# Moving a gate's logit into a projection's spare column, in a fused state-space and linear-attention kernel with a hand-ordered instruction list

## The chip, the cores and the metric

The kernel runs on one core of a Trainium2 chip. The metric is the device time of one execution in microseconds (us); the kernel is launched once per execution. The core has five instruction queues that run side by side and meet at semaphores: PE (matrix multiply), DVE (vector), ACT (scalar and table functions), POOL and SP (here a queue that issues DMA transfers).

## The reference

Two layers read the same kind of input and a gate mixes them, with `x` of 2048 positions by 512:

```python
g = sigmoid((x * gate_w).sum(-1, keepdims=True))
a = S5(x)              # h[t] = Lam_bar * h[t-1] + B_bar x[t];  y = 2 Re(C h) + x * Dskip
b = hedgehog(x)        # linear attention, 32 heads of 16
out = g * a + (1 - g) * b

# hedgehog: pq = q @ w_phi, pk = k @ w_phi (per head)
phi_q = cat(softmax(pq), softmax(-pq));  phi_k = cat(softmax(pk), softmax(-pk))
kv = phi_k^T v;  z = sum(phi_k);  o = (phi_q kv) / (phi_q z + 1e-6);  b = o @ wo
```

The two inputs `A_x` and the B layer's weights are bf16; the S5 layer has 512 complex states.

## The kernel before

**Tiles.** The 2048 positions lie in 16 tiles of 128; `order` gives the tile that step n of the output works on. `x` is kept transposed in `xT`. The weights of K and Q are folded with `w_phi` first (`st_W` transposes K's weight, `fold` multiplies, `st_f` for K and `st_w` for Q), so that one multiplication gives the features' logits, 15 relative columns for each of 32 heads, 480 in all.

**Steps.** Each step is a Python generator that issues a few instructions at each `next`: `k`, `v`, `q` project a tile (`tile_mm`, L483) and evict it from PSUM (`evac`: L129 on ACT, L131 on DVE); `x`, `n`, `e`, `s` (and `X`, `N`, `E`, `S` for Q) make the softmax features of a group of tiles on DVE and ACT (the exponential is L554); `S` ends with a transpose by DMA. `a` adds a tile to the K-V matrix in two PSUM banks that are held through it all (`live["acc"]`). `b`, `g`, `z`, `H`, `h`, `p`, `c` are the state-space layer: input products (L613, L625), the recurrence as a scan, and scalings (`scaled`: L436 on ACT, L438 on DVE). In the last third `y` multiplies states and C for a tile (L816), adding the skip term by a diagonal matrix `Dd` (L823), `o` makes numerator and denominator of the attention (L835, with a logarithm L839 and an exponential L842 for the division, and the multiplication L848), `O` transposes its result by DMA (L862), `t` multiplies by `wo` into the same bank as `y` and evicts it scaled by the gate (L875; L881 on ACT, L883 on DVE), and `R` stores it.

**The gate.** The logit of a tile is four matmuls of one column, with `gw_b` as the moving operand, into a spare column of the second K-V bank, issued with each tile of `a` (L603). After the last tile one step `G` makes the clamped, negated logit `nge` and the factor `G` (1 + exp) for all 16 tiles. `o` uses `nge` as a bias of its exponential (L842), `t` scales by `G`.

**The skip term.** For the tiles in `XD`, steps 8 to 14, it doesn't go through PE: `Ld` loads x untransposed into the space of K's and V's weights, `u` multiplies x by G and Dskip on DVE (L854), and `t` adds it (L879, on DVE).

**The order.** Nothing is scheduled by the machine: the string `ORDER` is a list of step names, and each name issues that step's next part. On each engine the instructions run in that order. `@` gives a step's PSUM banks (8 banks; `o` takes two neighbours), `:D` puts its eviction or scaling on DVE instead of ACT. A planner outside the kernel searched the list. `Z` is a matmul on zeros, of no use to the result. `Lk`, `Lx`, `Lv`, `Lq`, `Lb`, `Lc`, `Ld`, `Lo` issue loads from SP: K's weight, x, V's weight, Q's weight, B, C, the rows for `u`, and `wo`. `V` transposes the state-space parameters on PE (L321), `P` to `P4`, `M`, `U` and `i` work on them and make cosine and sine tables (`T2c`, `T2s`).

Of the kernel before, what the change touches and what calls it, by code (L numbers as in the profile page):

```python
# [10 lines left out]
ALU = mybir.AluOpType  # L11
AX = mybir.AxisListType
ACT = mybir.ActivationFunctionType
F32 = mybir.dt.float32
# [10 lines left out]
Lk Lk Z@0 B:D B Z Z Z Z Z B B W01@1 Lx Z W00@2 Lx W00 W00 W01 W01:D Lx W11@3 W10@4 W11 Z B f1@5 f1 Lv f0@1 T1@0 W10:D  # L25
f0:D T0@3 f2@2 T1 Lx T0:D f3@4 f3:D Lx f2 k1@6 Lx V@7 k0@3 V P k1 k1 U P U P2 Lx P2 U P2 P2 U P2 P4 P3 P4 k0 k0 n0 P4
x0 P P2 P3 i1 k2@7 k3@6 k2 k3 x0 i1 i1 x0 n0 i0 i1 i0 V2@3 V2 i1 M x0 k5@4 i0 k7@5 k7 i0 n0 k4@2 k4 x0 v1@6 k5 n0 i0
v1 i3 M k6@7 i3 x1 k6 i2 v5@2 i3 i3 i3 v5 i2 M v0@4 Lx Lx x1 Lb k8@5 n0 v0 i2 i2 i2 n1 L e0 x1 n1 x1 M gw v3@7 k15@4
n1 D v6@6 k15 Lb k9@2 v3 k8 b000@3 k11@0 k11 Lb b100@4 n1 x1 n1 b010@5 D x2 Lb s0 e1 n2 s0 n2 b100 Lq Lq b011@7 k10@0
b001@1 s0 x2 s0 s0 Lc b000 b101@3 x2 w3@4 k9 s0 n2 k13@2 x2 k10 b011 Lo n2 x2 n2 g001@7 M2 b010 b001 Lc e2 s1 x3 s1 n3  # L30
k14@5 x3 g000@1 v6 w1@0 s1 g001 x3 g000 n3 k13 s1 n3 g010@2 c1:D c1:D Lc Lc e2 g001 g010 s0 g000 s1 g011@6 g011 x0z:D
x3 n3 k14 c2 b101 D s1 s2 c2:D s2 g011 g010 g010 D g011 s2 a0@51 a0 c0 v2@7 w3 g011 g011 k12@3 c0:D w0@4 v2 g010 k12
g010 w2@6 w2 s2 g100@7 g100 x3 s2 n3 c3 c3:D x4 w1 Ld z0 z0 b110@6 x4 z0 n4 z0 w0 z0 n4 b111@2 g101@4 g101 s1 b110 z0
e3 g101 n4 q2@6 z0 n4 z0 q1@0 c3:D x4 z0 x4 e3 s3 z0 s3 g100 b111 c0 a1 a1 g111@4 s2 x4 n4 q3@3 g111 g111 g111 g110@2
H0:D g110 g110 q2 H0 c2 Ld Ld g110 s3 q0@6 b211@7 H0 s3 q1 s2 H0 g110 c0 q0 b201@0 q3 g110 c1 X0 N0 g111 g111 v7@6 H0
z1 z1 X0 s3 b200@2 g201@4 b201 N0 c2 v7 z1 X0 z1 z1 z1 s3 N0 b211 z1 b200 z1 g200@0 b210@6 g201 q4@7 e4 b210 X0 v4@2
# [12 lines left out]
S3 S3 y8 o10 p31 t8 o11@6 O3 t9 S3 S3 t6 o11 o11 p21 p31 t8 t9 y12@1 t7 p31:D y14@0 t6 t7 o11 o12@6 o12 p21 O5 p21
o13@2 u11 p31 y14 o12 o12 o13 y12 o13 R2 o14@6 o13 O6 o14 o14 o14 R4 u10 O7 y13@2 y13 o15@6 o15 o15 o15 t10 t10 R3 t11  # L50
t13 t11 u12 O8 u13 t12 t12 t13 u14 R5 t14 t14 R6 y15@54 y15 y15 t15 t15:D t15 R7 t15 R8 R8
# [4 lines left out]
XD = (8, 9, 10, 11, 12, 13, 14)  # L56
# [14 lines left out]
def kernel(  # L71
# [88 lines left out]
    Wq2 = const.tile([P, KT, DF], BF16, name="Wq2")  # L160
# [3 lines left out]
    gw_b = const.tile([P, KT], BF16, name="gw_b")  # L164
# [275 lines left out]
    def fold(W2, WT, dtile):  # L440
        pf = bank([P, DF], F32, "pf")
        for j in range(KT):
            MM(out=pf[:, j * DF // KT:(j + 1) * DF // KT], lhsT=WT[:, j, dtile * P:(dtile + 1) * P], rhs=BD[:, j].rearrange("p g f -> p (g f)"), start=True, stop=True)
        yield
        evac(W2[:, dtile, :].rearrange("p (hh f hl) -> p hh f hl", hh=8, f=Dh - 1), pf[:].rearrange("p (hh hl f) -> p hh f hl", hh=8, hl=4))
        yield
# [144 lines left out]
    def st_a(n):  # L591
        first, L = KGROUPS[n]
        for u in range(L):
            n_ = first + u
            ti = KO[n_]
            if n_ == 0:
                live["acc"] = [bank([P, 512], F32, f"kvacc{b}") for b in range(2)]
            for m in range(NB):
                MM(out=acc(m), lhsT=live["EE", n][:, u, m].rearrange("p s f -> p (s f)"),
                   rhs=vxb[n_ % NVX][:, 4 * m:4 * m + 4, :].rearrange("p h e -> p (h e)"),  # L600
                   start=(n_ == 0 and m % 4 == 0), stop=(n_ == NTI - 1), skip_group_check=True)
            for kt in range(KT):
                MM(out=live["acc"][1][:, 4 * KVW + ti:4 * KVW + ti + 1], lhsT=xT[:, kt, ti * P:(ti + 1) * P],  # L603
                   rhs=gw_b[:, kt:kt + 1], start=False, stop=(n_ == NTI - 1 and kt == KT - 1), skip_group_check=True)
            yield
# [137 lines left out]
    def st_G():  # L743
        VS(out=nge[:], in0=live["acc"][1][:, 4 * KVW:4 * KVW + NTI], scalar1=-Z_MAX, scalar2=-1.0, op0=ALU.max, op1=ALU.mult)
        yield
        aexp(out=G[:], in_=nge[:], func=ACT.Exp)
        yield
        VS(out=G[:], in0=G[:], scalar1=1.0, scalar2=None, op0=ALU.add)
        yield
        nc.vector.reciprocal(out=G[:], in_=G[:])  # L750
        yield
# [75 lines left out]
    def st_o(n):  # L827
        ti = order[n]
        op_ = pools["op"][1]
# [7 lines left out]
        yield  # L837
        ld = op_.tile([P, 2, 16], F32, name="ld")
# [3 lines left out]
        aexp(out=rd[:], in_=ld[:], func=ACT.Exp, scale=-1.0, bias=nge[:, ti:ti + 1])  # L842
# [8 lines left out]
    def st_u(n):  # L851
        ti = order[n]
        live["xd", n] = pools["op"][1].tile([P, D], F32, name="xd", bufs=2)
        nc.vector.scalar_tensor_tensor(out=live["xd", n][:], in0=xl(n), scalar=G[:, ti:ti + 1], in1=Drow[:], op0=ALU.mult, op1=ALU.mult)  # L854
        yield
# [10 lines left out]
    def st_t(n):  # L866
        ti = order[n]
# [5 lines left out]
        for py, (c, w) in zip(pys, [(0, D)] if len(pys) == 1 else LASTCUT):  # L873
            for g in range(HG):
                MM(out=py[:], lhsT=oT[:, g, :], rhs=Wo[:, g, c:c + w], start=False, stop=(g == HG - 1))  # L875
            yield
            ot = live["ot", g_][:, u, c:c + w]
            if n in XD:
                nc.vector.scalar_tensor_tensor(out=ot, in0=py[:], scalar=G[:, ti:ti + 1], in1=live["xd", n][:, c:c + w], op0=ALU.mult, op1=ALU.add)  # L879
            elif sel["eng"] == "act":  # L880
                nc.scalar.mul(out=ot, in_=py[:], mul=G[:, ti:ti + 1])  # L881
            else:
                VS(out=ot, in0=py[:], scalar1=G[:, ti:ti + 1], scalar2=None, op0=ALU.mult)  # L883
            yield

    def st_R(g):
# [3 lines left out]
        for (c, w), q in zip(LASTCUT if last else [(0, D)], (nc.sync, nc.scalar)):  # L890
# [4 lines left out]
          "M": st_M(), "M2": st_M2(), "D": st_D(), "L": st_L(), "G": st_G(), "Y": st_Y(), "END": st_END(), "Z": st_Z(), "x0z": st_x0(),  # L895
# [59 lines left out]
```

## Time and profile before

| | |
|---|---|
| median of 3 runs | 150.96 us (150.81 to 151.14) |
| the profiled execution | span 149.4 us from the first to the last instruction; no other time of this execution is given |
| PE, busy share | 142.8 us, 96%, 1010 matmuls |
| DVE | 139.0 us, 93%, 338 instructions |
| ACT | 125.1 us, 84%, 222 instructions |
| POOL | 26.6 us, 18%, 42 instructions |
| TensorE clock granted | 1.000 of full speed throughout |
| traffic | 20.14 MB in 52959 packets |

A row of the timeline gives the start, the duration of a run of like instructions, engine, line, operation, and what was written from what. An instruction's own record overlaps with the next one's on the same engine, so the time that it keeps its engine is better read from start to start. In a row of windows stand, after the bounds, the length and the busy time (with the number of instructions) of PE, its weight loads, DVE, ACT and POOL, then the granted clock, the DMA share and GB/s. In the chain of work that ended last a row is start, duration and what the chain ran through.

### The profile page before, as it was taken

How to read it: one execution, taken by the hardware profiler on the slowest of the kernel's cores; microseconds unless marked ns; L12 is line 12 of the kernel's file. 1: busy time of each engine (PE TensorE's matmuls, PEld its weight loads, DVE VectorE, ACT ScalarE, POOL GpSimd, SP SyncE). 2: the span in 40 equal slices, each digit the busy share in tenths (PEclk: the TensorE clock that was granted, in tenths of full speed). 3: DMA queues.
4: the chain of work that ended last, by engine and by line, in shares of the span. 5: the costliest groups of instructions: out<-in, count | busy, mean ns of one | idle time of the engine just before them, and what ended most of it. 6: DMA issues, size and time to landing. Idle time of an engine off the chain costs nothing.

```text
span 149.4 us, 2839 instructions
## 1 busy us (share of the span) xinstructions
PE 142.8 (96%) x1010; PEld 73.8 (49%) x1010; DVE 139.0 (93%) x338; ACT 125.1 (84%) x222; POOL 26.6 (18%) x42
## 2 busy tenths in 40 slices
PE   6999999999999999999999999999999999999980
PEld 2844444545545444464444467555444554455450
DVE  2899999999999999999999999999999999986880
ACT  3479999999999999999999999999989996552000
POOL 7403700000000341022605236011004200000000
PEclk9999999999999999999999999999999999999999
DMA  4999999991220174008274999908999996998742
GB/s 118 222 235 174 142 202 176 246 189 33 54 91 0 26 114 77 0 0 140 38 107 70 166 175 183 210 7 133 103 238 218 184 186 77 227 207 197 209 148 71
DMA packets 52959, 20.14 MB, mean 135 GB/s; under 512 B 44496, under 2 KB 52432, under 8 KB 52944
## 3 DMA queue, kind: packets, MB, share of 16 engines
q1 hardware_dynamic: 48000, 15.44, 53.1%
q0 software_dynamic: 4000, 4.20, 18.6%
q10 hardware_dynamic: 944, 0.31, 0.8%
q8 instruction: 8, 0.13, 0.4%
q14 instruction: 7, 0.06, 0.1%
HBM read 2.91 MB, written 2.10 MB: 33 GB/s over the span
## 4 chain that ended last, share of the span: by engine, by line
ACT 67%; PE 24%; issue 3%; DVE 2%
ACT EE L554 15%; PE PS L816 11%; ACT Xq L129 9%; PE PS L875 7%; ACT CT L436 6%; ACT vx L129 5%; ACT dg L436 4%; ACT H L129 3%; ACT vv L129 3%; ACT eb L129 3%; ACT Bn L129 3%; PE PS L316 2%; PE PS L835 2%; ACT lg L562 2%; ACT m L436 1%
## 5 line engine op out<-in xcount | busy, mean ns | idle before, releaser
L554 ACT ACTIVATE EE<-EE 128x2048 bf16<-128x2048 bf16 x16 | 32.5, 2066 | 0.2 <-DVE EE L548 0.2
L483 PE MATMUL PS<-WKV,xT 128*128 128x480 bf16 (+1 forms) x128 | 29.3, 373 | 0.2 <-DMA xT<-in_A_x_dram 0.2
L483 PEld LDWEIGHTS <-xT 128*128 128x128 bf16 x192 | 18.1, 98 | 19.4 <-DMA xT<-in_A_x_dram 0.7
L129 ACT CAST Xq<-PS 128x480 bf16<-128x480 f32 x32 | 20.1, 735 | 0.5 <-PE PS L483 0.5
L625 PE MATMUL PS<-xT,BT 128*128 128x512 bf16 x64 | 15.9, 379 | 0.0
L816 PE MATMUL PS<-C,H 128*128 128x512 bf16 x64 | 15.4, 378 | 0.5 <-DVE on L848 0.2
L875 PE MATMUL PS<-Wo,oT 128*128 128x512 bf16 (+2 forms) x68 | 15.5, 367 | 0.0
L613 PE MATMUL PS<-xT,BT 128*128 128x512 bf16 x64 | 15.4, 379 | 0.0
L483 PE MATMUL PS<-Wq,xT 128*128 128x480 bf16 x64 | 15.1, 366 | 0.0
L848 DVE TENSOR_TENSOR on<-PS,rd 128x512 bf16<-128x512 f32 x16 | 10.7, 681 | 2.3 <-ACT rd L842 2.3
L881 ACT ACTIVATE ot<-PS,G 128x512 bf16<-128x512 f32 (+1 forms) x8 | 4.9, 639 | 9.1 <-PE PS L875 9.1
L436 ACT ACTIVATE CT<-H,dgs 128x1024 bf16<-128x1024 bf16 x9 | 12.1, 1349 | 0.0
L129 ACT CAST vx<-PS 128x512 bf16<-128x512 f32 x16 | 11.7, 793 | 0.0
L648 POOL DMA_DIRECT2D C<-CT x4 | 5.4, 1352 | 35.0 <-ACT rc L566 31.8
L531 DVE TENSOR_TENSOR sm<-EE 128x2048 bf16<-128x2048 bf16 (+1 forms) x9 | 10.0, 1108 | 0.1
L542 DVE TENSOR_TENSOR EE<-Xq,mx 128x2048 bf16<-128x2048 bf16 (+1 forms) x9 | 10.0, 1109 | 0.0
L548 DVE TENSOR_TENSOR EE<-mn,Xq 128x2048 bf16<-128x2048 bf16 (+1 forms) x9 | 10.0, 1107 | 0.0
L613 PEld LDWEIGHTS <-BT 128*128 128x128 bf16 x64 | 6.3, 98 | 7.2 <-issue 0.2
L569 DVE TENSOR_TENSOR EE<-EE,rc 128x2048 bf16<-128x2048 bf16 x8 | 9.8, 1234 | 0.0
L625 PEld LDWEIGHTS <-BT 128*128 128x128 bf16 x64 | 6.1, 98 | 7.0
L875 PEld LDWEIGHTS <-oT 128*128 128x128 bf16 x68 | 6.1, 98 | 6.5 <-DMA oT<-on 0.5
L531 DVE TENSOR_TENSOR sm<-sm 128x512 bf16<-128x512 bf16 (+2 forms) x18 | 9.3, 516 | 0.0
(185 smaller groups left out, 325.8 us busy)
## 6 DMA issues: line engine op xcount, KB each, us to landing
out_dram<-ot SPq DMA_DIRECT2D x7, 256.0 KB, 2.4
C<-CT POOLq DMA_DIRECT2D x4, 256.0 KB, 3.9
eb<-CT POOLq DMA_DIRECT2D x4, 256.0 KB, 4.9
eb<-dg POOLq DMA_DIRECT2D x4, 256.0 KB, 5.9
WKV<-in_A_x_dram SPq DMA_DIRECT2D x3, 256.0 KB, 3.1
WKV<-in_B_wqkv_dram SPq DMA_DIRECT2D x1, 512.0 KB, 5.6
Wo<-in_B_wo_dram SPq DMA_DIRECT2D x1, 512.0 KB, 4.8
H<-CT POOLq DMA_DIRECT2D x2, 256.0 KB, 3.3
```

The lines of the kernel that those rows point to most:

```text
L129: nc.scalar.copy(out=out_ap, in_=in_ap)
L436: nc.scalar.mul(out=out_ap, in_=in_ap, mul=s_)
L483: MM(out=pt[:], lhsT=xT[:, kt, ti * P:(ti + 1) * P], rhs=W[:, kt, :], start=(kt == 0), stop=(kt == KT - 1))
L531: VT(out=dst, in0=cur[:, :, :, 0:n, :], in1=cur[:, :, :, n:2 * n, :], op=op)
L542: VT(out=half(EE, 0), in0=X5, in1=live["mx", p].to_broadcast([P, L, 8, Dh, 4]), op=ALU.subtract)
L548: VT(out=half(live["EE", p], 1), in0=live["mn", p].to_broadcast([P, L, 8, Dh, 4]), in1=X5, op=ALU.subtract)
L554: aexp(out=EE[:, l_:l_ + 2], in_=EE[:, l_:l_ + 2], func=ACT.Exp)
L613: MM(out=pb[:], lhsT=BT[:, ri, kt, j * P:(j + 1) * P], rhs=cells(kt, 2 * pr), start=(kt == 0), stop=(kt == KT - 1))
L625: MM(out=pgq[:], lhsT=BT[:, ri, kt, js], rhs=cells(kt, r1), start=(kt == 0), stop=False)
L816: MM(out=py[:], lhsT=hs[j][ri], rhs=C2[:, 1 - ri, j, c:c + w], start=(j == 0 and ri == 0), stop=False)
L848: VT(out=live["on", g_][:, u], in0=pn[:, :, :, 0:Dh], in1=rd[:].unsqueeze(3).to_broadcast([P, 2, 16, Dh]), op=ALU.mult)
L875: MM(out=py[:], lhsT=oT[:, g, :], rhs=Wo[:, g, c:c + w], start=False, stop=(g == HG - 1))
```

## The change

The gate's weight becomes a 481st column of Q's folded weight, so that the logit of a tile comes out of `q`, in the same bank, and is evicted by itself into `nge` (one column; an extra part of step `q`). `a` loses its four small matmuls. `G` becomes four steps, each for four tiles. `nge` and `G` are indexed by the step's number instead of the tile's. `XD` becomes the steps 8 to 11: steps 12, 13 and 14 get their skip term by `Dd` on PE again, lose `u`, and their `t` is a plain scaling. `ORDER` is a new list throughout, with other places, banks and engines for most steps.

```diff
-XD = (8, 9, 10, 11, 12, 13, 14)
+XD = (8, 9, 10, 11)
-    Wq2 = const.tile([P, KT, DF], BF16, name="Wq2")
+    Wq2 = const.tile([P, KT, DF + 4], BF16, name="Wq2")
     def st_gw():
-        nc.vector.tensor_copy(out=gw_b[:], in_=vec[:, 4, :])
+        nc.vector.tensor_copy(out=Wq2[:, :, DF], in_=vec[:, 4, :])
...
     def st_q(n):
-        pq = bank([P, DF], F32, "pq")
+        pq = bank([P, DF + 1], F32, "pq")
         tile_mm(pq, order[n], Wq2)
         yield
-        evac(xrel(n), pq[:].rearrange("p (hh x) -> p hh x", hh=8))
+        evac(xrel(n), pq[:, 0:DF].rearrange("p (hh x) -> p hh x", hh=8))
+        yield
+        evac(nge[:, n:n + 1], pq[:, DF:DF + 1])
         yield
...
     def st_a(n):
-            for kt in range(KT):
-                MM(out=live["acc"][1][:, 4 * KVW + ti:4 * KVW + ti + 1], lhsT=xT[:, kt, ti * P:(ti + 1) * P],
-                   rhs=gw_b[:, kt:kt + 1], start=False, stop=(n_ == NTI - 1 and kt == KT - 1), skip_group_check=True)
...
-    def st_G():
-        VS(out=nge[:], in0=live["acc"][1][:, 4 * KVW:4 * KVW + NTI], scalar1=-Z_MAX, scalar2=-1.0, op0=ALU.max, op1=ALU.mult)
-        yield
-        aexp(out=G[:], in_=nge[:], func=ACT.Exp)
+    def st_G(g):
+        ns = slice(4 * g, 4 * g + 4)
+        VS(out=nge[:, ns], in0=nge[:, ns], scalar1=-Z_MAX, scalar2=-1.0, op0=ALU.max, op1=ALU.mult)
+        yield
+        aexp(out=G[:, ns], in_=nge[:, ns], func=ACT.Exp)
...
```

The start of the list, and the place where the first outputs are made, before (-) and after (+):

```diff
-Lk Lk Z@0 B:D B Z Z Z Z Z B B W01@1 Lx Z W00@2 Lx W00 W00 W01 W01:D Lx W11@3 W10@4 W11 Z B f1@5 f1 Lv f0@1 T1@0 W10:D
-f0:D T0@3 f2@2 T1 Lx T0:D f3@4 f3:D Lx f2 k1@6 Lx V@7 k0@3 V P k1 k1 U P U P2 Lx P2 U P2 P2 U P2 P4 P3 P4 k0 k0 n0 P4
+Z@0 Z Lk Z Z B W01@1 Z Z Lx B Lk B W00@2 W10@3 W11@4 V@5 Lv W10 W11 Lx V W01 B W00 P B P U T0@3 P2 f3@4 W00 W01 Z
+T1@2 f0@5 Z U P2 Lx Lx U P2 T1 P2 f2@1 U P2 P f1@6 P4 v1@0 f0:D f3 f2 P4 f1:D P4 k1@4 T0:D k2@6 k1 k0@3 P2 i1 P3 i1
+i1 i0 P3 i1 i0 k0 i1 Lq k1 Lx k0 i0 Lq M k4@1 i0 v1 M i0 k3@4 i2 M x0 i2 Lx n0 i3 n0 v5@3 Lx k4 x0 V2@0 x0z Lx k6@5
...
+k3 k7@4 i2 n0 k8@1 k9@2 k2 k6 v5 x0 i2 x0 w0@3 V2 n0 Lb M2 k5@5 i3 x0 w2@6 n0 x1 gw Lb M i2 k10@0 x1 i3 n1 k8 x1 n1
+k12@1 x1 k7 w0 D n1 i3 k9 k5 w3@5 b100@2 n1 i3 x1 L Lb e0 k11@3 k12 Lc b000@4 b000 g000@7 k10 x2 D b010@1 Lb x2 n1
...
+X3 t0 y3@3 o3 S1 p20 E2 N3 y4@0 G2 E2 p00 y4 t0 G1 X3 N3 S2 t1 S1 O1 y3 N3 o4@4 p30 o5@1 G1 S2 y4 G1 o4 N3 y3 S2 o5
...
+u11 o15@0 o15 R3 y15@76 o15 y15 t11 y15 o15 y14 t12 R5 t13 t14 t12 t14:D t13 O8 t15 t15 R6 R7 t15 t15:D R8 R8
```

Read engine by engine, the two lists differ in this way: PE has 64 matmuls of one column fewer and 12 more with `Dd`; ACT has 245 instructions instead of 222, among them the 16 one-column evictions, four exponentials of the sigmoid instead of one, ten 512-wide output scalings instead of seven and all four evictions of K's transposed weight instead of two; DVE has 340 instead of 338, with three fewer `u`, and 12 instead of 3 for the sigmoid. SP issues the same loads less the last two of x for `u`, but in another order: V's weight before x's second block, Q's weight between the first x pairs, the last x pair after B.

More of the change, by code (lines that the diff above doesn't have):

```diff
@@ new lines @@
+t5 o6 o6 p30 E3 o7 y7 S2 p30 p10 t4 y8@5 p20 p01:D p20 E3 S2 y6 y10@6 p01 p20 O3 o8@1 p30 o8 p30 o8 S3 y8 t4 o8 S3
+p01 t7 G3 p11 p11 S2 o9@0 y10 t6 o9 G2 S3 S3 G2 y11@2 o9 o9 p31:D t5 o10@0 S3 S3 R1 y11 S3 y9@7 o10 y9 p21:D S3 o10
+p21 t6 o10 p21 G2 O4 S3 t7 o11@0 p21 u8 G3 t9 p31 o11 t8 p11 S3 y12@4 p31 p21 p31 y14@3 o11 o11 p31 o12@0 o12 y12
+y14 o12 u9 t8 o12 o13@0 y13@5 G3 t9 y13 u10 R2 y13 S3 o13 o13 G3 O5 o13 o14@0 y12 t10 o14 O6 R4 o14 o14 t11 O7 t10
+u11 o15@0 o15 R3 y15@76 o15 y15 t11 y15 o15 y14 t12 R5 t13 t14 t12 t14:D t13 O8 t15 t15 R6 R7 t15 t15:D R8 R8
@@ L841, in st_o @@
         rd = op_.tile([P, 2, 16], F32, name="rd")
[L842 removed]
+        aexp(out=rd[:], in_=ld[:], func=ACT.Exp, scale=-1.0, bias=nge[:, n:n + 1])
         yield
```

69 lines of the change are left out of this document (28 added, 41 removed).

## The prediction

> **What bounds the kernel now.** I read the page first (share of each engine, the chain), then the windows, to see which engines are full in which stage, then the chain and the timelines of ACT, PE, DVE and SP.
>
> ```profile
> span 149.4 us, 2839 instructions
> ACT 67%; PE 24%; issue 3%; DVE 2%
> 90.00:100.00 10.00, 10.00 (x119) 6.01 (x116) 10.00 (x23) 10.00 (x16) 2.44 (x2) 1.00 0.78 146
> 120.00:130.00 10.00, 9.65 (x79) 4.83 (x78) 9.93 (x19) 7.49 (x18) 0.00 (x0) 1.00 0.93 160
> 9.55 1.02 ACT Xq L129 x2
> 109.76 0.42 PE PS L835 x8
> 145.11 0.62 DVE ot L883
> ```
>
> In 90 to 100 us PE, DVE and ACT (third, fifth and sixth column) are all full; in 120 to 130 only PE and DVE are. The chain is two thirds ACT: it enters ACT with the first eviction of a K tile at 9.55 us and leaves it near 103; from 121 it is PE's list without a break. So work taken off one engine is worth little by itself. The time is set by when each full list starts, how long it is up to the place where another engine waits for it, and the end. I follow two such places: tile 1's output eviction on ACT, and the matmuls of `o4` on PE (109.76 now). The median of the runs is 150.96, 1.5 us over the profiled span; I add the shift of the end to the median.
>
> **PE's list gets shorter by 0.9 us.**
>
> ```profile
> 46.23 0.24 PE L603 MATMUL PS<-gw_b,xT 128*128 128x1 bf16 x4
> 46.33 0.41 PE L599 MATMUL PS<-vx,EE 128*128 128x68 bf16 x8
> 106.95 0.22 PE PS L823 x4
> ```
>
> Four gate matmuls hold PE from 46.23 to 46.33, 0.025 each: 64 go, -1.6 us. Tiles 12 to 14 get their skip term back on PE: 12 matmuls at 0.055, +0.7. The 481st column of 64 matmuls is under 0.03 in all. If nothing else moved, this alone would be 150.1.
>
> **DVE's list gets shorter by some 3 us, mostly into slack.**
>
> ```profile
> 140.58 1.40 DVE L854 SCALAR_TENSOR_TENSOR xd<-WKV,G,Drow 128x512 f32<-128x512 bf16 x2
> 141.90 1.40 DVE L879 SCALAR_TENSOR_TENSOR ot<-PS,G,xd 128x512 bf16<-128x512 f32 x2
> 9.28 0.17 DVE L362 TENSOR_SCALAR ssm_par<-ssm_par 128x4 f32<-128x4 f32 x1
> ```
>
> Three `u` and three `t` go, each 0.66 from start to start (140.58 to 141.90 holds two): -4.0. The sigmoid in four parts adds nine small instructions, at most 0.17 each: +1.5 at most. A few scalings change sides and nearly cancel. The gain lies after 115 us for the most part, where PE's list is what lasts; I count nothing for it.
>
> **ACT's list, from the first K eviction to tile 1's output.**
>
> ```profile
> 108.49 1.24 ACT L881 ACTIVATE ot<-PS,G 128x512 bf16<-128x512 f32 x2
> 97.13 0.42 ACT L839 ACTIVATE ld<-PS 128x32 f32<-128x32 f32 x1
> 97.21 0.80 ACT L129 CAST Xq<-PS 128x480 bf16<-128x480 f32 x1
> 91.39 1.46 ACT L436 ACTIVATE n<-H,dgs 128x1024 bf16<-128x1024 bf16 x1
> 92.42 1.33 ACT L129 CAST Xq<-PS 128x480 bf16<-128x480 f32 x2
> 112.65 1.93 ACT L436 ACTIVATE dg<-H,dgs 128x512 bf16<-128x512 bf16 x3
> 114.49 0.17 ACT L839 ACTIVATE ld<-PS 128x32 f32<-128x32 f32 x1
> 10.69 1.28 ACT L136 ACT_TABLE_LOAD   x1
> 13.18 0.42 ACT L136 ACTIVATE T2s<-psi 128x256 bf16<-128x256 f32 x1
> 13.49 0.50 ACT L136 ACTIVATE T2c<-kk,hpi_t 128x256 bf16<-128x256 f32 x1
> ```
>
> Now it takes from 9.55 to 109.06 (the second of the pair at 108.49, 0.57 each): 99.5 us, with hardly an idle moment. In the new list this stretch loses what is done ahead of it: a table load (1.28), one sine and one cosine table (0.31 and up to 0.50) and three tiny activations (about 0.5), -2.5. It loses to DVE, or to later, one 1024-wide scaling (1.03, as 91.39 to 92.42) and four 512-wide ones (0.61 each, three in 112.65 to 114.49), -3.5. It gains one 1024-wide and one 512-wide scaling, +1.6; one exponential of the sigmoid, +0.1; and the 16 gate evictions. No row shows a one-column eviction; the nearest is the logarithm of 32 columns from PSUM, which holds ACT 0.08 from 97.13 to 97.21 when work is queued behind it, and 0.42 in its own record. Between 0.08 and 0.42 I take 0.10, near the start-to-start time, since ACT is full: +1.6. Sum -2.7: 96.8 us.
>
> [...]
>
> **But that stretch starts later.** What is done ahead of it must be done first.
>
> ```profile
> 5.10 1.23 ACT L129 COPY Xq<-PS 128x512 bf16<-128x512 bf16 x2 [1.96 <-PE PS L299]
> 4.00:8.00 4.00, 3.94 (x43) 3.22 (x42) 3.57 (x15) 2.37 (x5) 1.56 (x4) 1.00 1.06 232
> 4.21 0.43 PE PS L316
> 7.92 0.65 DVE L131 CAST WKV<-PS 128x480 bf16<-128x480 f32 x1
> 7.59 0.41 DVE L131 COPY xT<-PS 128x512 bf16<-128x512 bf16 x1
> 11.42 0.35 DVE L456 TENSOR_SCALAR kk<-iot,ssm_par 128x256 f32<-128x256 f32 x1
> 11.88 0.48 DVE L460 SCALAR_TENSOR_TENSOR psi<-iot,ssm_par,kk 128x256 f32<-128x256 f32 x1
> 12.88 0.29 DVE L464 TENSOR_SCALAR kk<-psi 128x256 uint32<-128x256 uint32 x1
> L156 POOL DMA_DIRECT2D vec_n<-in_A_log_dt_dram x1: 518/518/518, 2.8 to 2.8; - x1
> DMA to landing us min/median/max: 3.7/4.1/4.3
> ```
>
> All four transposed quarters of K's weight are now evicted by ACT (two were DVE's), 0.6 each from about 5.2, with the first exponential between them: done at 7.8. Ahead of the folds on PE stands `T1`, which needs x's second block, now queued on SP behind V's half megabyte: 0.64 MB at the 232 GB/s of that window is 2.8 us, so about 7.5. Then f0, a warm-up matmul (0.43), f2 and f1, folds of four short matmuls at some 0.055 each: 8.9. On DVE the last fold eviction (0.65), an x tile (0.41), kk (0.35), psi (0.48) and the absolute value (0.29), with another kk between, less 0.1 at each step since the next starts before the record ends: about 11.4; on ACT then the cosine table (0.4 to 0.5): the first K eviction starts at 11.8. And `V`, now ahead of half of the weight's transposes in PE's list, waits for the parameters: issued at 2.8, landing 3.7 to 4.3 later, at 6.5 to 7.1, where the list reaches it at 5.7. That can push all by another 1.1, to 12.9. I take 12.3: 2.75 later than now. V's first matmuls would start at 9.0 to 9.9 where K's start at 7.9 now, so PE loses 1.0 to 2.0 as well, which is more than its 0.9.
>
> **SP's queue.** Q's weight (two transposes) moves ahead of three x pairs and of B; the last x pair moves behind.
>
> ```profile
> L230 SPq DMA_TRANSPOSE BT<-in_A_B_re_dram x2: 1807/1980/2152, 15.0 to 16.8; - x2
> L230 SPq DMA_TRANSPOSE BT<-in_A_B_im_dram x2: 1302/1302/1302, 19.0 to 20.4; - x2
> DMA to landing us min/median/max: 3.7/4.4/5.3
> 21.91 1.03 PE L613 MATMUL PS<-xT,BT 128*128 128x512 bf16 x4
> ```
>
> B_re's second half was the ninth transpose (issued 16.8) and becomes the tenth, the place that is issued at 19.0 now: it lands at 22.7 or later. The first `b` ran at 21.91; it now has 18.7 us of PE work ahead of it, 1.2 less, so PE reaches it at 20.9 to 22.2 and waits up to 1.8, with its eviction behind on ACT, and again at B_im (thirteenth transpose, +1.3 on the same reckoning). ACT's part in this is 0 to 1.5; I take 0.5, since PE's late start covers much of it.
>
> [...]
>
> **The sum.** Tile 1's output eviction starts at 12.3 + 96.8 + 0.5 = 109.6 and ends at 110.2. `o4` takes banks 4 and 5, and bank 5 is tile 1's; so PE starts `o4` at 110.2, 0.4 later than now. PE's own list agrees: 1.0 less work ahead of `o4`, 1.0 to 2.0 lost at the start: 109.8 to 110.8. From `o4` to its end PE has 0.1 more than now. At the end:
>
> ```profile
> 145.33 0.37 ACT L881 ACTIVATE ot<-PS,G 128x128 bf16<-128x128 f32 x1 [6.71 <-PE PS L875]
> 137.62 0.42 PE L835 MATMUL PS<-KVm,phT 128*128 128x68 bf16 x8
> 144.25 1.05 PE L875 MATMUL PS<-Wo,oT 128*128 128x384 bf16 x8
> ```
>
> The last piece is now the 128-wide one on DVE instead of 384 wide (0.62): -0.2. But `o15` and `t15`, 6.6 us apart now (137.62, 144.25; eviction, division, transpose by DMA between), have only 5.0 of PE work between them in the new list, `t10`, `t11` and others having gone ahead: a wait of up to 1.6, less what the transpose gains when fewer stores stand before it. I take 0.5. Sum 0.4 + 0.1 - 0.2 + 0.5 = +0.8: 151.8 us.
>
> **Rivals.** *The early start pays (faster).* x and the parameters land 0.8 earlier than I reckon, B in time, a gate eviction costs 0.08, and DVE's 3 us shorten the waits behind 110 us. First eviction 11.5, no extra idle: tile 1 ends at 11.5 + 96.5 + 0.6 = 108.6, and PE reaches `o4` at about 109.2, -0.6; with the end's -0.2 and shorter late waits (another -0.2): 150.0. For it: 0.9 us less on PE, 3 on DVE. Against: DMA is already full in the first 30 us.
>
> *B arrives late (slower than the forecast).* The whole price falls on ACT and PE: +1.5 instead of 0.5, and the next load too: 153.0. It decides from a landing of B_re after 22.2.
>
> *t15 waits its full 1.6:* 152.9.
>
> *No change:* the start costs PE just the 0.9 it is spared: 151.0.
>
> **How the numbers follow.** Forecast case 0.38 (151.3 to 152.3), early start 0.27, late B 0.15, late t15 0.10, no change 0.10. A measurement of this kernel tells about 0.2%, 0.3 us. Faster by more: the early start, most of it: 0.26; within: no change and a little of the forecast's edge, 0.13; slower: the rest, 0.61. The range leaves a tenth on either side: a little under the early start, and the two late cases partly together: 149.9 to 153.8.
>
> **What would show it.** First K eviction near 12.3 us (11.5: the rival); PE waiting for BT near 22; 16 small ACT rows with starts 0.08 to 0.12 apart; tile 1's `ot` on ACT near 109.6 with PE waiting for it at L835; PE's row from o15 to t15 broken by a DMA wait on oT. If the first K eviction is before 11.5, or PE reaches `o4` before 109.4, the forecast is wrong.

## The result, and the profile after

The changed kernel takes 160.81 us (median of 4 runs, 159.43 to 161.27), against 151.05 for the kernel before on the same chip: ratio 1.0618, 95% interval 1.0564 to 1.0673, or 9.8 us slower by the medians. The forecast was 0.8 us slower, with a range up to 153.8: the sign was right, the size far off. (Executions of some of the kernels below fall into two groups 2 to 5 us apart; ratios compare the lower groups.)

The page of the profiled execution (160.39 us). Line numbers are those of each run's own kernel: L130, L556, L815, L832, L871 and L877 are what was L129, L554, L816, L835, L875 and L881 before.

```profile
span 158.7 us, 2746 instructions
PEclk9999999999999999999999999999957999999999
ACT 49%; PE 31%; DMA 12%; issue 2%; DVE 2%; POOL 1%; POOLq 0%
ACT EE L556 14%; PE PS L483 8%; PE PS L815 8%; PE PS L871 6%; DMA phT<-EE 6%; ACT Xq L130 5%; ACT vx L130 4%; ACT CT L436 4%; DMA vec_n<-in_A_log_dt_dram 3%; DMA oT<-on 3%; ACT vv L130 3%; ACT H L130 2%; ACT Bn L130 2%; PE PS L611 2%; PE PS L832 2%
```

Before, the chain was ACT, then PE. Now 12% of it are transfers: `phT` and `oT`, the two kinds of transposes by DMA, and the parameters `vec_n`. And for the first time the clock dips (slices 30 and 31).

The places that the prediction named, from the timelines of ACT and PE:

```profile
14.71 1.22 ACT L130 CAST Xq<-PS 128x480 bf16<-128x480 f32 x2
111.41 0.69 ACT L877 ACTIVATE ot<-PS,G 128x512 bf16<-128x512 f32 x1
7.87 0.16 PE L321 MATMUL PS<-ident,vec_n 12*128 12x12 bf16 x1 [1.04 <-DMA vec_n<-in_A_log_dt_dram]
11.67 4.67 PE L483 MATMUL PS<-WKV,xT 128*128 128x512 bf16 x20
24.16 1.03 PE L611 MATMUL PS<-xT,BT 128*128 128x512 bf16 x4
116.57 1.09 PE L832 MATMUL PS<-KVm,phT 128*128 128x68 bf16 x16 [4.32 <-DMA phT<-EE]
118.30 3.38 PE L871 MATMUL PS<-Wo,oT 128*128 128x512 bf16 x8
```

The first K eviction starts at 14.71 (9.55 before, 12.3 forecast), tile 1's output eviction at 111.41 (109.06 before, 109.6 forecast), `o4` at 116.57 (109.76 before, 110.2 forecast). `o4` does not wait for a bank: it waits 4.32 us for the transposed features of tile 4. The eight matmuls behind it at 118.30 take 3.38, where the eight such at 106.91 took 1.89. From `o4` to the end of the span are 42.1 us (158.7 - 116.57), against 39.6 before. So of the 9.3 us by which the span grew, 6.8 are there when `o4` starts and 2.5 come behind it.

SP's timeline shows that this transpose was issued at 107.32, right after its input was ready (before: 104.44), so it took 9.2 us. What else was in flight is seen in the windows around it (last column: GB/s moved; the one ahead of the last two is the granted clock), in the transfers of 107 to 117 us, and in the queues' rows of 112 to 116 (packets, MB, share of 16 DMA engines; q0 carries GpSimd's transfers, q1 those of SP):

```profile
110.00:111.00 1.00, 1.00 (x6) 0.42 (x5) 1.00 (x4) 1.00 (x2) 0.00 (x0) 1.00 1.14 209
112.00:113.00 1.00, 0.25 (x2) 0.00 (x0) 1.00 (x4) 1.00 (x2) 0.00 (x0) 1.00 1.64 82
113.00:114.00 1.00, 0.00 (x0) 0.00 (x0) 0.88 (x5) 0.14 (x1) 0.00 (x0) 1.00 1.30 105
114.00:115.00 1.00, 0.00 (x0) 0.00 (x0) 0.00 (x0) 0.00 (x0) 0.00 (x0) 0.74 1.31 126
115.00:116.00 1.00, 0.00 (x0) 0.00 (x0) 0.00 (x0) 0.00 (x0) 0.00 (x0) 0.50 1.33 111
116.00:117.00 1.00, 0.43 (x8) 0.43 (x9) 0.00 (x0) 0.00 (x0) 0.00 (x0) 0.50 1.18 261
...
q0 software_dynamic: 544, 0.52, 47.6%
...
eb<-CT POOLq DMA_DIRECT2D x1, 256.0 KB, 9.8
phT<-EE SPq DMA_TRANSPOSE x2, 7.4
...
q1 hardware_dynamic: 909, 0.22, 85.3%
q0 software_dynamic: 210, 0.20, 54.2%
```

From 112 to 116 us the DMA engines are full (share above 1) and yet move 82 to 126 GB/s; at 110, and again at 116, they move 209 and 261. In between two kinds of transfers move side by side: the transposes issued by SP, and accumulating transfers issued by GpSimd, 0.52 MB in all (`eb<-CT`, the first additions of the steps `p01` and `p11`, at 105.7 and 106.5 us), of which the second took 9.8 us. (At 110 it is in flight as well, but next to nothing of it moves: 2 packets in 110 to 111.) PE, DVE and ACT stand still at the end of it, and the clock falls to half.

### The profile page after: what moved, and what is told of

It reads as the page before. It is cut to its first block, busy times and chain, and to the rows that moved or that the text cites. A ratio compares the mean times of both kernels' runs of the same rounds, so it can differ in the third digit from the quotient of the medians.

```text
span 158.7 us, 2746 instructions
## 1 busy us (share of the span) xinstructions
PE 143.9 (91%) x942; PEld 74.9 (47%) x958; DVE 135.5 (85%) x340; ACT 129.0 (81%) x245; POOL 30.2 (19%) x42
## 4 chain that ended last, share of the span: by engine, by line
ACT 49%; PE 31%; DMA 12%; issue 2%; DVE 2%; POOL 1%; POOLq 0%
ACT EE L556 14%; PE PS L483 8%; PE PS L815 8%; PE PS L871 6%; DMA phT<-EE 6%; ACT Xq L130 5%; ACT vx L130 4%; ACT CT L436 4%; DMA vec_n<-in_A_log_dt_dram 3%; DMA oT<-on 3%; ACT vv L130 3%; ACT H L130 2%; ACT Bn L130 2%; PE PS L611 2%; PE PS L832 2%
## 5 line engine op out<-in xcount | busy, mean ns | idle before, releaser
L556 ACT ACTIVATE EE<-EE 128x2048 bf16<-128x2048 bf16 x16 | 31.0, 1976 | 0.0
L130 ACT CAST Xq<-PS 128x480 bf16<-128x480 f32 x32 | 19.3, 639 | 0.2
L871 PE MATMUL PS<-Wo,oT 128*128 128x512 bf16 (+2 forms) x65 | 16.3, 393 | 1.2 <-DMA oT<-on 1.0
L815 PE MATMUL PS<-C,H 128*128 128x512 bf16 x60 | 15.1, 379 | 0.9 <-ACT nge L130 0.7
L483 PE MATMUL PS<-Wq,xT 128*128 128x481 bf16 x64 | 15.4, 366 | 0.1
L837 ACT ACTIVATE ld<-PS 128x32 f32<-128x32 f32 x16 | 3.0, 222 | 13.1 <-PE PS L832 13.1
L877 ACT ACTIVATE ot<-PS,G 128x512 bf16<-128x512 f32 (+1 forms) x11 | 7.3, 671 | 4.7 <-PE PS L871 4.7
L832 PE MATMUL PS<-KVm,phT 128*128 128x68 bf16 x128 | 6.8, 201 | 4.3 <-DMA phT<-EE 4.3
L871 PEld LDWEIGHTS <-oT 128*128 128x128 bf16 x68 | 6.6, 104 | 8.3 <-issue 1.7
L130 ACT CAST vx<-PS 128x512 bf16<-128x512 f32 x16 | 10.4, 663 | 0.0
L646 POOL DMA_DIRECT2D eb<-dg x4 | 5.9, 1486 | 22.0 <-ACT lg L564 11.7
L832 PEld LDWEIGHTS <-phT 128*128 128x128 bf16 x128 | 6.2, 102 | 7.5 <-DMA phT<-EE 4.8
```

The lines of the kernel that those rows point to most:

```text
L130: nc.scalar.copy(out=out_ap, in_=in_ap)
L556: aexp(out=EE[:, l_:l_ + 2], in_=EE[:, l_:l_ + 2], func=ACT.Exp)
L646: nc.gpsimd.dma_start(out=out_ap, in_=in_ap, accum_op=ALU.add)
L815: MM(out=py[:], lhsT=hs[j][ri], rhs=C2[:, 1 - ri, j, c:c + w], start=(j == 0 and ri == 0), stop=False)
L832: MM(out=pn[:, hf, 4 * m:4 * m + 4, :].rearrange("p h e -> p (h e)"), lhsT=ph[:, 4 * hf + m, :], rhs=KVm[:, 4 * hf + m, :], start=(m == 0) ...
```

## The experiments

They test three terms: the late start, the transposes beside accumulating transfers ("adds" below), and the clock; against the rivals that the edit itself, or late work on DVE and ACT, is the loss. A wait in a row of waits is its total, how often, and the longest. In the diffs, tokens of the list stand for steps.

**Moving the two adds back (e1).**

```diff
-o1 p11 o2@3 N2 p01 y5@7 ... S1 X3 o4
+o1 o2@3 N2 y5@7 ... S1 p01 p11 X3 o4
```

> Edit: the changed kernel, with the first scalings of p11 and p01 (two 1024-wide ACT instructions, and so the two accumulating transfers that follow them) moved behind the last step of S1. Theory (mixed transfers): in the changed kernel the transpose of tiles 4 and 5 took 9.21 us, against 5.26 before, because two accumulating transfers issued 1.6 and 0.9 us ahead of it ran beside it. Moved away, it is issued near 107.3 and lands by 112.6 to 113.2, PE waits under 1.2 us at o4, the granted clock stays 1.0, and the time is 160.8 - 3.9 - 2.4 = 154.5 (153.5 to 155.5). Rival (late list): the transpose is late because the work ahead of it is late, and its length is its own; it still takes 8 us or more and the time is 160 to 161.

Measured: 160.34 us, ratio 1.0604 (1.0569 to 1.0640). From PE's timeline, its waits in 100 to 130 us, the windows, and the transfers of 105 to 113:

```profile
112.37 0.67 PE L832 MATMUL PS<-KVm,phT 128*128 128x68 bf16 x16
...
PE PS L871 <- DMA oT<-on: 3.5, 1, 3.5
...
111.00:112.00 1.00, 1.00 (x7) 0.46 (x5) 1.00 (x3) 1.00 (x4) 0.00 (x0) 1.00 1.14 219
...
phT<-EE SPq DMA_TRANSPOSE x2, 4.3
```

The mechanism holds: without the adds beside it, the same transpose took 4.3 us, the engines moved 219 GB/s, and `o4` started at 112.37 without a wait, with the same three transposes on SP's queue. But the time did not fall. The adds, now issued at 114.6 and 115.7, met the next transpose (`oT`, issued at 117.2, 6.7 us), PE waited 3.5 us there, and the clock dipped there instead (mean granted clock 0.989 over the 158.6 us; at half speed that is some 3.5 us, an estimate). Not all of this is theirs: a third add, issued at 117.3, and a read of instructions at 118.7 (see e16) fell on that `oT` too. The sum in the expectation took for granted that the adds cost nothing in their new place.

**Moving them ahead (e17).**

```diff
-X2 o0@3 h3 ... p11 o2@3 N2 p01 y5@7
+X2 p01 p11 o0@3 h3 ... o2@3 N2 y5@7
```

> Edit: the changed kernel with the first scalings of p01 and p11 ahead of the eviction steps of o0 in ACT's list, some 3 to 5 us earlier, where e1_adds_later put them later. Theory (an accumulating transfer slows the transposes that it meets): both run near 101 to 105 us, ahead of the transpose of tiles 4 and 5, which then lands 4.3 to 5.5 us after its issue; PE waits at o4 under 1.5 us, no dip of the clock there; 155.3 (154 to 156.5), if the transpose oT issued at 103.7 does not pay for it. Rival (the collision only moves, to this oT or to what ACT now does 2.2 us later): 159 to 161.

Measured: 159.24, ratio 1.0485 (1.0437 to 1.0534), the rival's time. The transpose again took 4.3 us, but was issued at 110.16: ACT did 2.1 us of scalings ahead of evictions that PE was waiting for, and the clock fell to half behind that wait. From PE's waits in 98 to 130 us, and a window:

```profile
PE PS L815 <- ACT nge L130: 2.8, 1, 2.8
PE PS L871 <- DMA oT<-on: 1.4, 1, 1.4
...
106.00:108.00 2.00, 2.00 (x17) 1.16 (x15) 2.00 (x6) 0.30 (x2) 0.00 (x0) 0.50 0.97 146
```

**Leaving the adds out (e8, e19).** The changed list has five adds of stage `p` behind 105 us (105.7, 106.5, 119.8, 130.3, 132.6); the old list has two (114.3, 115.0).

```diff
-            add_by_dma(E_, t1)
+            if pr == 0:
+                add_by_dma(E_, t1)
...
-            add_by_dma(E_, t2)
+            if (j, pr) == (0, 0):
+                add_by_dma(E_, t2)
```

> Edit: the changed kernel, with five accumulating transfers of the stage p left out (the second one of p10 and both of p01 and p11: those that were issued at 105.7, 106.5, 119.8, 130.3 and 132.6 us); the ACT scalings that feed them stay. So the even output positions lack those terms. Theory (accumulating transfers beside transposes slow both, and the waits for them are the loss behind 105 us): the transpose of tiles 4 and 5 lands 4 to 5 us after its issue, no transpose behind it takes over 5.5 us, PE waits at o4 under 1.2 us and under 1 us at each later transpose, the clock stays 1.0, and the time is 160.8 - 4.0 - 2.4 - 0.9 = 153.5 (152.5 to 154.8). Rival (the transposes are late by the order of DVE and ACT work): 157.5 or more.

For e19, only the first hunk of this diff:

> Edit: the changed kernel, with only the first accumulating transfers of p01 and p11 left out, the two that were issued at 105.7 and 106.5 us; the three later ones stay. Theory (these two make the wait at o4, 4.3 us, and the dip of the clock with it): the transpose of tiles 4 and 5 lands 4.3 to 5 us after its issue, PE waits at o4 under 1.2 us, the clock stays 1.0 there, and the time is 155.0 (154 to 156.5); the other 2 us up to the 153.0 of e8_no_late_adds belong to the three later ones. Rival (the three later ones stretch their transposes the more when PE comes earlier, as in e1_adds_later): 157.5 or more.

Measured: 153.04, ratio 1.0144 (1.0115 to 1.0173), without all five; without the first two alone 156.34 (154.9, 155.0, 157.7 and 158.1), ratio 1.0241 (1.0148 to 1.0334). The windows and the transfers of the first, at the place shown above:

```profile
112.00:113.00 1.00, 1.00 (x23) 0.86 (x22) 1.00 (x4) 1.00 (x2) 0.00 (x0) 1.00 1.00 180
113.00:114.00 1.00, 1.00 (x11) 0.58 (x9) 1.00 (x6) 1.00 (x6) 0.00 (x0) 1.00 1.16 215
...
phT<-EE SPq DMA_TRANSPOSE x2, 4.3
```

The engines are full, the clock is 1.00, and transposes move at up to 215 GB/s. The five adds are worth 7.8 us by the medians (160.81 - 153.04), 7.2 by the ratios (0.0474 of 151); the first two alone 5.7 by the ratios (0.0377 of 151).

**The kernel before without its two late adds (e14).**

> Edit: the kernel before, with the two accumulating transfers issued at 114.3 and 115.0 us left out (the second ones of p11 and p01), so tiles 12 to 15 lack a term; the scalings stay. It is the measure for e15_gate_no_adds. Theory (in the kernel before these two run behind one transpose and ahead of the next and cost next to nothing): 150.2 to 151.2. Rival (they cost the kernel before as much as they cost the changed one): 149 or less.

Measured: 151.44, ratio 1.0005 (0.9988 to 1.0021). In the old list these two adds cost nothing that can be measured. The trace of the kernel before shows one difference. They were issued at 114.3 and 115.0, beside the transpose of 113.62, but none of their packets moved ahead of 117, when that transpose was almost through. From its transfers of 114 to 117, of 117 to 118 and of 118 to 120 us:

```profile
q1 hardware_dynamic: 2298, 0.58, 107.2%
...
q0 software_dynamic: 87, 0.09, 64.1%
q1 hardware_dynamic: 348, 0.09, 44.5%
...
q0 software_dynamic: 345, 0.34, 119.4%
```

So there the two kinds mostly took turns, at 193, 176 and 173 GB/s. Why they took turns there, and not in the changed kernel, is not shown.

**One add pulled ahead in the kernel before (e7).**

> Edit: the kernel before, with three scalings on ACT (the last two pieces of p11 and p01, 1.8 us) and so the two accumulating transfers that were issued at 114.3 and 115.0 moved ahead of the first transpose of tiles 4 and 5, which is issued at 104.4 now and up to 1.8 later then. Theory (accumulating transfers beside transposes): the transpose takes 8 us or more instead of 5.3, o4 starts at 113 to 116 instead of 109.8, PE stands idle for 3 us or more and the clock falls to half for 3.4 or 6.8 us; the time is 154 to 158, less what is gained where the two transfers are missing at 114. Rival (the transposes have their own length): landing in 5 to 6 us, o4 at 110 to 111.6, 151 to 152.8.

Measured: 152.59, ratio 1.0101 (1.0085 to 1.0118): the rival's range. Steps of `p01` go in order, so only the add of `p11` moved, to 102.8; that of `p01` went out at 110.4. The transpose took 5.7 us and PE waited 0.4 for it. The add at 102.8 landed at 107.7, 2.5 us behind the issue of the transpose, and cost it little. This did not reproduce the collision from the other side.

**PE kept busy through the wait (e2).**

```diff
-y3 N3 o4@4
+y3 N3 Zd@4 Zd ... (20 times) o4@4
```

> Edit: the changed kernel, with 20 warm-up matmuls of 512 columns (4.3 us of PE) into bank 4 just ahead of o4, where PE stood idle for 4.3 us; nothing reads them. Theory (the idle cuts the clock): o4 still starts near 116.6, the granted clock stays at 1.0, the 4.7 us that PE then ran at half speed give back 2.4 us: 158.4 (157.8 to 159.0). Rival (the dip costs nothing, since ACT or DVE sets the pace after 116, or it has another cause): 160 to 161, with or without the dip.

Measured: 159.90, ratio 1.0599 (1.0548 to 1.0649); from PE's timeline, the windows, and its waits in 120 to 150 us:

```profile
112.50 4.48 PE L317 MATMUL PS<-warm 128*128 128x512 bf16 x20
116.86 0.68 PE L833 MATMUL PS<-KVm,phT 128*128 128x68 bf16 x16
117.83 1.89 PE L872 MATMUL PS<-Wo,oT 128*128 128x512 bf16 x8
...
118.00:120.00 2.00, 2.00 (x11) 0.90 (x10) 1.98 (x6) 2.00 (x5) 0.28 (x1) 1.00 0.92 250
...
PE PS L872 <- DMA oT<-on: 1.9, 2, 1.7
```

So the idle does cut the clock: with PE busy it stays at 1.00, and the eight matmuls take 1.89 instead of 3.38. But of the 2.4 us only 0.9 came out by the medians, 0.3 by the ratios, whose intervals overlap: the two kernels are not told apart. PE, earlier now, waited 1.9 us for later `oT` transposes where it had waited 1.0. So what the dip itself was worth in the time is 0 to 0.9 us here.

**The start (e3, e4, e18).**

```diff
-W10@3 W11@4 V@5 Lv W10 W11 Lx V W01 B W00 P B P U T0@3 P2 f3@4 W00 W01 Z T1@2 f0@5
+W10@3 W11@4 Lv W10 W11 Lx W01 B W00 W00 W01 T0@3 B f3@4 V@5 V P P U P2 Z T1@2 f0@5
```

> Edit: the changed kernel, with V behind all transposes of K's weight and behind f3 in PE's list, and the first exponential of P behind the last two of their evictions on ACT. Theory (V's wait and the exponential hold up the folds): the first matmul of v1 moves from 11.67 to 9.5 (9.2 to 10.0), the first K eviction from 14.7 to 12.5, tile 1's output eviction from 111.4 to 109.2; the slow transpose and the dip of the clock stay, so the time falls by 2.2 to 158.6 (158.0 to 159.5). Rival (a later wait takes the gain back: x or B not landed): 160 to 161.

> Edit: both the earlier start and the moved accumulating transfers (the edits of e3_start and e1_adds_later together). Theory (mixed transfers, clock and start are three separate terms): 160.8 - 3.9 - 2.4 - 2.2 = 152.3 (151.3 to 153.5). Rival (late list): 158 to 159, as e3_start.

> Edit: e8_no_late_adds (five late accumulating transfers left out) with the earlier start of e3_start. Theory (late start and collisions are separate terms, and DVE's additions took the difference in e11_adds_on_dve): 153.0 - 1.6 = 151.4 (150.8 to 152.0), the level of the kernel before. Rival (the later list has no use for an earlier start once the transposes are in time): 153.

Measured: e3 159.16, ratio 1.0527 (1.0497 to 1.0558); e4 158.85, ratio 1.0505 (1.0477 to 1.0532); e18 151.73, ratio 1.0051 (1.0016 to 1.0085). From ACT's timeline of e3:

```profile
13.82 0.56 ACT L130 CAST Xq<-PS 128x480 bf16<-128x480 f32 x1
110.67 0.69 ACT L877 ACTIVATE ot<-PS,G 128x512 bf16<-128x512 f32 x1
```

The first matmul of `v1` moved from 11.67 to 10.75 and the first K eviction by 0.9, less than half of what was expected: `V` still waited for the parameters, until 8.20, and `T1` and three folds stood behind it. In the time it was worth 1.4 us by the ratios, both with the five adds (1.0618 - 1.0527) and without them (1.0144 - 1.0051). e4 missed as e1 did: `o4` started at 110.99, and PE lost it again at the next transposes (4.2 us of waits for `oT`). e18 is within its range.

**Adding on DVE and on GpSimd (e11, e12, e13).**

```diff
-add_by_dma(E_, t1)
+VT(out=E_, in0=E_, in1=t1, op=ALU.add)    # e12: nc.gpsimd.tensor_tensor; so for t2
```

> Edit: e3_start, with the five late accumulating transfers of stage p replaced by five additions on DVE (128x1024, some 0.6 us each) at the same places of the list; the output is complete. Theory (those transfers are the loss behind 105 us and DVE has room for 3.0 to 3.4 us more there): as e8_no_late_adds, less the 1.6 us that the earlier start brought: 151.6, up to 1 us more if DVE's additions stand in the way: 151.6 to 152.6. Rival (DVE is the bound there): the additions cost their whole time, 154.5 to 155.

> Edit: as e11_adds_on_dve, but the five additions are computed by GpSimd, which is idle there. Theory (the transfers are the loss): 151.3 to 152.5, whatever engine adds. Rival (GpSimd's additions slow DVE's instructions beside them or come too late for y8 and y12): 153 or more, with DVE rows beside them longer than in e11_adds_on_dve.

> Edit: as e11_adds_on_dve, with a further rebuilt start: x's second block loaded ahead of V's weight, all four folds ahead of V and of the parameters' work, the matmuls and evictions of k1 and k2 ahead of v1 and of the sines, two more warm-up matmuls. Theory (the start is worth its whole length): first K eviction 10.0 to 11.0 us, 1.5 to 2.5 earlier than in e3_start, and the time 1 to 2 us under e11_adds_on_dve: 149.8 to 151. Rival (later waits for x, B or the sines take it back): as e11_adds_on_dve, within 0.5.

Measured: e11 153.86, ratio 1.0182 (1.0152 to 1.0212); e12 161.49, ratio 1.0660 (1.0595 to 1.0725); e13 154.71, ratio 1.0255 (1.0204 to 1.0305). A window of e11, then the same of e18, then POOL and DVE in e12:

```profile
115.00:125.00 10.00, 8.62 (x59) 4.14 (x59) 10.00 (x17) 8.80 (x15) 0.00 (x0) 1.00 1.04 171
```

```profile
115.00:125.00 10.00, 9.06 (x68) 4.64 (x69) 9.59 (x18) 9.38 (x16) 0.00 (x0) 1.00 1.07 186
```

```profile
104.81 5.65 POOL L770 TENSOR_TENSOR eb<-eb,CT 128x1024 bf16<-128x1024 bf16 x2 [13.01 <-ACT ld L843]
105.86 2.62 DVE L583 TENSOR_TENSOR EE<-EE,rho 128x1024 bf16<-128x1024 bf16 x1
```

DVE (fifth column) is full with the additions (10.00) and only nearly so without them (9.59): they cost 2.1 us (153.86 - 151.73) of their 3, five of some 0.6 from start to start. e11 computes the whole output, and is 5.2 us faster by the ratios than e3, which has the five adds as transfers (1.0527 - 1.0182). GpSimd takes 2.8 us for one, and a DVE instruction of 0.68 (so a like one at 111.06, with GpSimd idle) takes 2.62 beside it; what slows it no row shows. In e13 the first K eviction came at 11.71, 2 us before e3's, and the kernel was no faster: the next ones waited for the sines behind it.

**The edit in the old list (e5, e9, e10, e15).** After's code with before's list; each gate eviction right behind its Q eviction.

```diff
-q5@2 q5 ... G ... G ... G ... G
+q5@2 q5 q5 ... G0 G1 ... G2 G0 G1 G2 ... G3 G3 G0 G1 G2 G3 ... G0 G1 G2 G3      # e5; e9: XD 8 to 11 as well
+q5@2 q5 q5 ... G0 G1 ... G2 ... G3 G0 G1 G2 ... G0 G1 G2 G0 G1 G2 G3 ... G3 G3   # e10, e15
```

> Edit: the kernel before, its list and its seven skip terms on DVE kept, with the gate logit as column 481 of Q's weight and the sigmoid by four tiles alone: each eviction of the gate column stands right behind its Q eviction, and the four parts of the sigmoid stand where the one stood. Theory (the edit itself costs next to nothing, the new list does): PE loses 1.6 us of matmuls, ACT gains 16 evictions of 0.06 = 1.0, DVE thirteen small instructions of 0.07 to 0.1: 151.4 (150.4 to 152.4). Rival (the evictions of one column hold banks and ACT, and the edit itself is slow in any list): 154 or more.

> Edit: as e5_gate_only, and the skip term on DVE for tiles 8 to 11 alone: all of the change but its new list. Theory (the list is the loss): PE has 0.7 us more than in e5_gate_only near the end, two small loads fewer in SP's queue near 92 us: 151.8 (150.6 to 152.8). Rival (the edit is slow in any list): 155 or more.

> Edit: as e5_gate_only, but the exponentials of the sigmoid stand on ACT, and the steps behind them on DVE, some 6 to 10 us later in the lists (where the gate is first needed), and only the clamps early. In e5_gate_only ACT stood still for 2.1 and 1.7 us in front of two of these exponentials, DVE and PE with it. Theory (the gate column itself costs next to nothing, what e5_gate_only lost were these waits and the collision of transfers that they led to): 151.4 (150.4 to 152.4). Rival (the evictions of one column cost the time in any list): 154 or more.

> Edit: e10_gate_late_sigmoid (the old list with the gate column) with the same two transfers left out. Theory (the gate column itself costs next to nothing; what e10_gate_late_sigmoid lost behind 114 us is the collision of transfers): within 0.7 of e14_before_no_adds, 150.3 to 151.9, with the transpose issued near 115 landing in under 6.5 us instead of 9.7. Rival (the edit costs by its own instructions): 153 or more.

Measured: e5 157.96, ratio 1.0426 (1.0369 to 1.0484); e9 159.81, ratio 1.0558 (1.0507 to 1.0609); e10 155.65 (153.3, 154.9, 156.5 and 157.3), ratio 1.0193 (1.0117 to 1.0268); e15 152.54, ratio 1.0078 (1.0058 to 1.0098). My theory failed for e5 and e9, where I had put the sigmoid's exponentials too early, and ACT stood behind them (timeline of ACT, e5):

```profile
96.82 0.20 ACT L745 ACTIVATE G<-nge 128x4 f32<-128x4 f32 x1 [1.74 <-DVE nge L743]
109.49 0.20 ACT L745 ACTIVATE G<-nge 128x4 f32<-128x4 f32 x1 [1.62 <-DVE nge L743]
```

These two runs are thus no measure of the edit. e10, without such waits, reaches `o4` at 110.22 (109.76 before), but misses its 151.4 as well. Its profiled execution (156.45, above those that the ratio takes) loses time where its two adds meet a transpose: the one issued at 114.81 took 9.7 us, against 5.1 in the kernel before with the adds at the same distance behind it. (In e5 the one issued at 119.11, with its adds at 119.75 and 120.48, took 8.3.) With these two adds left out (e15) it takes 5.3, and the kernel 152.54. Beside e14, that prices the gate column in the old list at 1.1 us (152.54 - 151.44), a little over the bound I had set, and not at 9.8. It does so with all seven skip terms on DVE: what moving three of them costs in the old list no run shows, since only e9 has that.

**The read of instructions (e16).** In e10 one more thing fell on the transposes. Windows of e10 and its transfers of 113 to 118 us:

```profile
115.00:116.00 1.00, 1.00 (x5) 0.49 (x5) 1.00 (x2) 0.97 (x4) 0.55 (x1) 1.00 2.40 54
116.00:117.00 1.00, 0.95 (x6) 0.41 (x5) 1.00 (x2) 1.00 (x2) 1.00 (x2) 1.00 0.07 7
117.00:118.00 1.00, 1.00 (x9) 0.59 (x8) 1.00 (x3) 1.00 (x2) 0.88 (x1) 1.00 1.14 204
...
q8 instruction: 1, 0.02, 2.0%
```

One 16 KB read of the instruction queue started at 114.6; in the two microseconds from 115 on the transposes then in flight moved 54 and 7 GB/s.

```diff
+Zt@2 Zt ... (14 times, one column each) k9@2
```

> Edit: e10_gate_late_sigmoid with 14 matmuls of one column (0.4 us of PE in all; nothing reads them) in front of k9, near 20 us. In all traces a 16 KB read of the instruction queue comes once per 125 or so matmuls; in e10_gate_late_sigmoid the one at 114.5 us fell on the transpose oT issued at 113.4, whose packets stood still for 1.9 us. 14 matmuls more move this read some 2 us ahead, to 112.6, between two transfers. Theory (the read stops the transposes that it meets): the oT issued near 113.4 lands in 3.1 to 3.6 us instead of 4.7, the phT behind it by 121.5 instead of 124.5, and the time is 152.5 (151 to 153.8). Rival (the reads do not matter, the accumulating transfers alone do): 155 to 156 again.

Measured: 152.6, 152.8, 157.7 and 157.8 us; ratio 1.0086 (1.0055 to 1.0117). In the profiled execution (152.84) the read started at 113.8, between two transfers, the `oT` landed in 3.6 us instead of 4.7, the `phT` behind it at 122.4 instead of 124.5, and PE waited 1.0 us for it instead of 3.1. But e15 parts the two causes better. Its read started at 114.4, close to that of e10, and its windows show the same standstill (53 GB/s in 115 to 116, 82 in 116 to 117). Yet without the two adds its `oT` landed in 4.4 us, the `phT` in 5.3, and the kernel took 152.54. So in both runs transposes all but stood still beside such a read (7 to 82 GB/s), but the 9.7 us of e10 needed the adds. What a read costs beside adds is not settled.

## Why the prediction was wrong, step by step

*The sum up to tile 1's output: right in the middle, wrong at its start.* ACT's stretch from the first K eviction to tile 1's output was 96.7 us (14.71 to 111.41), forecast 96.8. That it fits to 0.1 is partly luck: the gate evictions took some 0.8 less than reckoned, and about as much went to short gaps between other instructions, for which the sum had no term. The first K eviction is the step that failed: 14.71 instead of 12.3 (11.8 to 12.9). Three parts were mis-sized. The parameters landed at 7.7, not 6.5 to 7.1, and PE stood for them until 7.87. The prediction had all four evictions of K's weight done at 7.8, with the first exponential between them: but that exponential needs `V`, so the last two evictions stood behind it on ACT and ended at 9.68. And the transposes and folds went at half speed: four matmuls of 128 columns took 0.40 from start to start (7.96 to 8.36), 0.1 each, where eight took 0.44 in the kernel before (6.82 to 7.26). (The windows give a granted clock of 1.00 there, so no view shows the reason.) e3, which undoes less than half of it, puts 1.4 us on that.

*Gate evictions:* start to start 0.05 on average (56.44 to 56.49 for the first; 0.85 for all sixteen), not 0.10 (1.6). The 0.08 from start to start of the row that stood for them (97.13 to 97.21) would have been nearer. In the old list the first output eviction came 0.85 later with them (109.34 in e15, 108.49 before).

*Late B:* did not happen. B_re's second half landed at 22.7, as reckoned (and past the 22.2 that was to decide for this rival), but `b` ran at 24.16 without a wait; PE came later than B.

*`o4`:* this is the step that lost the most. The prediction took bank 5 as the only thing `o4` waits for. It has a second input, the transposed features, and in the kernel before these had landed at 109.69, 0.07 us ahead of `o4`: there was no slack to lose, and the prediction has no term for it. In the changed kernel the bank came free at 112.1, as 2 us of late start would have it, and the transpose at 116.5. Its length was never questioned: 5.3 became 9.2, because the list puts two adds 1.6 and 0.9 us ahead of it. The prediction followed SP's queue at the start only, and GpSimd's not at all. Of the 6.8 us by which `o4` came later, 2.3 are the bank's and 4.4 the transpose's. By e8 all the adds behind 105 us are 7.2 to 7.8 us, the clock in it.

*From `o4` to the end:* +0.4 forecast, +2.5 measured. The granted clock was half from about 114.5 (0.74 in 114 to 115) to 121.3 in the changed kernel, 6.8 us, of which PE worked in the last 4.7 and so lost 2.4. That idle cuts the clock e2 shows: 1.00 in 114 to 118 with PE busy, 0.50 to 0.74 without. In the changed kernel it fell 2.2 us after PE had stopped (112.25 to 114.47), and it was down too behind waits of 2.8 us in e17 (granted clock 0.50 in 106 to 108) and of 2.1 in e5 (0.59 in 102 to 104). So these waits of 2 to 4 us cost the clock behind them and had to be priced with that, though e2 got back no more than 0.9 us of the 2.4. The 0.5 for `t15` was not spent: it ran behind `y15` without a wait for a transfer.

*DVE's slack:* less than was said. 3 us more on DVE cost 2.1 (e11).

*The rivals:* none named it. "Late B" had the right kind of cause, a transfer that lands late, in the wrong place.

What is shown: the five late adds are worth 7.2 to 7.8 us in the new list and two of them nothing in the old one, the part of the late start that e3 undoes 1.4; both out, the kernel is within 0.8 us of the one before (e18, 151.73), near the 1.1 us of the gate column in the old list. That the adds cost it by slowing transposes beside them is seen in the traces (9.2 us against 4.3); moving two of them got back 2 us at most (e1, e17), leaving them out (e8, e19) or adding on DVE (e11) most of it. What is not shown: why adds and transposes move side by side in the new list and take turns in the old one, and why they are then slower than either alone. No version here that computes the whole output beat the kernel before.

## What to carry to other kernels

For each step, list all that it waits for with the time at which each came, and not only what came last: an input that lands 0.07 us ahead of its reader is on the critical path too. When a list is reordered, follow the transfers of every queue beside one another, not only the engines; a transfer off the path can slow one that is on it (here a transpose took 9.2 us beside two adds and 4.3 without them), and moving it helps little where it meets the next one (6.7 us for `oT` in e1). And price a wait of PE of 2 us or more with the clock that it may cost behind it (here 0.50 to 0.59 behind waits of 2.1 to 4.3 us).

## What the runs showed of the hardware

- In windows with full DMA engines, transposes by DMA alone moved 180 to 261 GB/s (e8, 112 to 113; the changed kernel, 116 to 117), and accumulating transfers from GpSimd alone 141 (there, 108 to 109) to 173 (the kernel before, 118 to 120). Side by side they moved 82 to 126 in the changed kernel (112 to 116), under both; but not always: 169 there in 109 to 110, and 176 in the kernel before in 117 to 118. If the two kinds only shared the engines, the sum should lie between their own figures above (an estimate from these), as in the last two; why it was 82 to 126 no run shows.
- A 16 KB read of the instruction queue (8 in the kernel before, with 1010 matmuls, 7 in the changed one, with 942) held up the transposes in flight for a microsecond or two in some windows: they moved 54 and 7 GB/s in 115 to 117 in e10, 53 and 82 in e15, and 54 in 107 to 108 in the kernel before. There, windows around the read at 106.75 us:

```profile
106.00:107.00 1.00, 1.00 (x9) 0.53 (x8) 1.00 (x3) 1.00 (x1) 0.00 (x0) 1.00 1.18 224
107.00:108.00 1.00, 1.00 (x9) 0.50 (x6) 1.00 (x4) 1.00 (x2) 0.00 (x0) 1.00 1.87 54
```
